# Pair 1 of an attention kernel loaded by tokens on GpSimd's queue, pair 0's x on the hardware queues, and all small tables from one diagonal

## The chip, the cores and the metric

The kernel runs on one core of a Trainium2 chip. The metric is device time in microseconds (us), lower is better. Three runs of the kernel before gave 121.71, 122.49 and 123.0; the median, 122.49, is the time before. A profile is one further execution, recorded by the hardware profiler.

The core has engines that run side by side, each with its own queue of instructions in program order: TensorE (matmul; PE in the profile, its weight loads PEld), VectorE (DVE), ScalarE (ACT), GpSimd (POOL) and SyncE (SP). Transfers between memory and the core are carried by 16 DMA engines. SyncE and ScalarE issue them to hardware queues (q1 and q10 in the profile), GpSimd to a software queue (q0); only GpSimd's transfers change the type on the way.

## What is computed

```python
batch, n_heads, seq, head_dim, d_state = (4, 8, 768, 32, 16)      # x, a, B, C
n_tokens, d_model, d_ff = (3072, 256, 1536)                       # w_a, w_b, w_out
...
    for c in range(nc):
        ...
        cum = np.cumsum(la, axis=-1)
        L = np.exp(cum[:, :, :, None] - cum[:, :, None, :])
        causal = np.arange(chunk)[:, None] >= np.arange(chunk)[None, :]
        L = L * causal
        CB = np.einsum('bhin,bhjn->bhij', Cc, Bc)
        M = CB * L
        y_intra = np.einsum('bhij,bhjd->bhid', M, xc)
        decay_to_i = np.exp(cum)
        y_inter = np.einsum('bhin,bhnd->bhid', Cc, state) * decay_to_i[:, :, :, None]
        y[:, :, sl] = y_intra + y_inter
        ...
        state = decay_full[:, :, None, None] * state + np.sum(Bx, axis=2)
...
    a = x @ w_a
    b = x @ w_b
    return (a * b @ w_out).astype(np.float32)
```

A linear attention with decay (state space form), whose output y, its heads side by side, is the input of a bilinear feed-forward layer. All inputs and the output are float32.

## The kernel before, in words

The sequence of 768 is cut into 6 blocks of 128 tokens, the batch of 4 into 2 pairs of sequences (bt is 0 or 1 within one). A *pair* p stands for block p // 2 and sequences 2(p % 2) and 2(p % 2) + 1, so there are 12 pairs. Each pair goes through these stages:

- Loads of B, C and x into the tiles bn, cn and xn (`load1`, `load2`, lines 134 to 154). For pairs below P0 = 4 a partition holds two neighbouring tokens of one sequence: partitions 0 to 63 are sequence 0, 64 to 127 sequence 1, and each load is two transfers with runs of 128 bytes (B, C) or 256 bytes (x). From pair 4 on a partition is a token ("by token"); runs are 64 bytes for B and C, 128 for x, and one transfer takes both sequences.
- `scale_bc` (line 314) multiplies B and C by the decay factors fB and fC, giving bm and cm in float16. `transposes` or, for pair 1, `transposes1` turn them on TensorE into BT and CT; from pair 4 on a DMA turns them. `scale_x` makes a float16 copy of x.
- `scores` (line 414) multiplies BT by CT into PSUM; `mask` (line 464) multiplies by the causal table while it copies to T1, three quarters on VectorE and one on GpSimd (there ScalarE copies out of PSUM first). The two-token layout uses the table `causal`, the by-token one `causal_q`.
- `pv_u` (line 477) and `ds_mm` (line 505) multiply by x to the output and the state sums. Pair 0's output goes by `evac0`, the others' by `pv`, to X2T, the input of the feed-forward layer.

The feed-forward layer of a pair runs in six units (`unit_mm`, line 658, for Wa and Wb, 256 columns a matmul; `evac_a` copies Wa's result; `times` multiplies), then by Wo. Units of the first pairs are interleaved with the next pairs' stages. From block 2 on both pairs of a block share units of 512 columns (`bunit`, line 735).

The decays come from `scan` (running product of a within a block), `over_mid` (reciprocal of its middle), `sel_over_mid`, and `factors_mm` (line 266), small float32 matmuls by the table `sel` that lay the factors out on the partitions.

Nothing is scheduled automatically: each engine's order is the program's order. Line 180 on issues the loads: a, B and C of pairs 0 and 1 by SyncE and ScalarE; then the tables are made, `sel`, `ident`, `headm` and `causal` by GpSimd's affine selects (lines 198 to 236), with reduces and copies on VectorE. Behind these on GpSimd's queue stand x of pair 0, the first half of Wa, the first quarter of Wb (lines 237 to 240) and x of pair 1; the rest of Wb's first half and the second halves of Wa and Wb follow at lines 855 and 856, after GpSimd's `scale_bc` of pair 1 and its `mask` of pair 0. The weights are cast to float16 on the way. Pair 2's inputs and Wo follow on the same queue (lines 878 to 885), pair 3's on SyncE after the second half of Wb (line 921). `warmup` (line 244) issues matmuls on zeros, whose result isn't used, while TensorE would otherwise wait at the start. `units_mm` runs the first two units of pair 0 with Wa, first both on the first half of X2T, then both on the second. PSUM banks of the pool `psf` are given out by the string BANKS, in the order of the calls.

Of the kernel before, what the change touches and what calls it, by code (L numbers as in the profile page):

```python
# [10 lines left out]
f32 = mybir.dt.float32  # L11
# [11 lines left out]
    "01232013201321023102310231023102301230120312031201320132013201320132031023102310213203120"  # L23
    "3120310213021302130210321032103210321032103210321302130213021302130213021302130213021302"
# [4 lines left out]
def kernel(  # L29
# [13 lines left out]
    nc = tc.nc  # L43
# [31 lines left out]
    zero = big.tile([BH, Q], f32, name="zero")  # L75
# [12 lines left out]
    warm = big.tile([128, 512], f16, name="warm")  # L88
# [41 lines left out]

    def by_token(t_):
        return t_.rearrange("p h r n -> p (h r n)").rearrange("p (t h n) -> p t h n", t=2, h=H)

    def load1(eng, p, which, bt, i0=0, n=64):
        blk, bp = divmod(p, NBP)
        if p >= P0:
            return eng.dma_start(
                by_token(pair_in[p][which])[:, bt],
                (B, C, x)[which][2 * bp + bt, :, blk * Q : (blk + 1) * Q, :].rearrange("h q n -> q h n"),
            )  # L140
# [6 lines left out]
    def load2(eng, p, which):  # L147
        if p < P0:
            return [load1(eng, p, which, bt) for bt in range(2)]
# [6 lines left out]
    def load_w(half):  # L156
        c = slice(half * KC, (half + 1) * KC)
        return [
            nc.gpsimd.dma_start(W[half], src.rearrange("(f p) e -> p f e", p=128)[:, :, c])
            for W, src in ((Wa, moe_w_a), (Wb, moe_w_b))  # L160
        ]

    def load_w0(which, part):
        W, src = ((Wa, moe_w_a), (Wb, moe_w_b))[which]
        w = (KC, KC // 2)[which]
        t_ = W[0][part] if which else W[0]
        nc.gpsimd.dma_start(t_, src.rearrange("(f p) e -> p f e", p=128)[:, :, part * w : (part + 1) * w])
# [13 lines left out]
    for p_ in range(3):  # L181
# [4 lines left out]
    load1(nc.sync, 0, 1, 0, 0, 32)  # L186
    load1(nc.scalar, 0, 1, 0, 32, 32)
    load1(nc.sync, 1, 0, 0)
    load1(nc.scalar, 1, 0, 1)
    load1(nc.sync, 1, 1, 0)  # L190
    load1(nc.scalar, 1, 1, 1)
    nc.scalar.preload_act_table_set("natural_log_exp_and_others")
    nc.vector.memset(warm.bitcast(u32), 0)
    nc.vector.memset(ident, 1.0)
    nc.vector.memset(headm, 1.0)
    nc.vector.memset(causal, 1.0)
    nc.vector.memset(zero, 0.0)
    nc.gpsimd.memset(sel, 1.0)
    nc.gpsimd.affine_select(
        out=sel,  # L200
        in_=sel,
        compare_op=ALU.is_equal,
        fill=0.0,
        base=0,
        pattern=[[-H, 2], [-2 * H, NBP], [-1, H]],
        channel_multiplier=1,
    )
    nc.gpsimd.affine_select(
        out=ident, in_=ident, compare_op=ALU.is_equal, fill=0.0, base=0, pattern=[[-1, 128]], channel_multiplier=1
    )  # L210
# [7 lines left out]
    nc.vector.tensor_copy(indm.rearrange("p (h n) -> p h n", n=N), of_h.unsqueeze(2).broadcast_to((BH, H, N)))  # L218
    for base, step in ((0, 1), (N - 1, -1)):
        nc.gpsimd.affine_select(  # L220
            out=headm,
            in_=headm,
            compare_op=ALU.is_ge,
            fill=0.0,
            base=base,
            pattern=[[-N * step, H]],
            channel_multiplier=step,
        )
    nc.vector.tensor_reduce(
        out=par, in_=headm.rearrange("p (m e) -> p e m", e=2), op=ALU.add, axis=mybir.AxisListType.X  # L230
    )
    for bt in range(2):
        v = causal[64 * bt : 64 * bt + 64]
        nc.gpsimd.affine_select(  # L234
            out=v, in_=v, compare_op=ALU.is_ge, fill=0.0, base=0, pattern=[[-1, 2], [1, Q]], channel_multiplier=-2
        )
    for bt in range(2):
        load1(nc.gpsimd, 0, 2, bt)
    load_w0(0, 0)
    load_w0(1, 0)  # L240
    for bt in range(2):
        load1(nc.gpsimd, 1, 2, bt)

    def warmup(n, bank, cols=512):
        for _ in range(n):
            nc.tensor.matmul(
                bank[:, 0:cols], warm[:, 0:128], warm[:, 0:cols], start=True, stop=True, skip_group_check=True
            )


    def scan(lo, hi):
        for k in range(lo, hi):
            nc.vector.tensor_tensor_scan(Pr[:, k], a_sb[:, k], zero, 1.0, ALU.mult, ALU.add)
# [12 lines left out]
    def factors_mm(lo, hi, fps=None, k0=0):  # L266
        if fps is None:
            fps = bank("fps")
        w = 2 * NBP * H
        F = fps[:, k0 * w : (k0 + hi - lo) * w].rearrange("p (k r c) -> p k r c", k=hi - lo, r=2)  # L270
        for k in range(lo, hi):
            for r in range(2):
                for bt in range(2):
                    nc.tensor.matmul(
                        F[64 * bt : 64 * bt + 64, k - lo, r],
                        Pr[:, k].rearrange("p (i r) -> p r i", r=2)[:, r],
                        selr[:, k, bt],
                        start=True,
                        stop=True,
                        skip_group_check=True,  # L280
                        tile_position=(0, 64 * bt),
                    )
        return F.rearrange("p k r c -> p (k r c)")

# [29 lines left out]
    def scale_bc(p, which, eng, factor=None):  # L314
        blk, bp = divmod(p, NBP)
        name, f = (("bm", fB), ("cm", fC))[which]
        raw = by_token(pair_in[p][which]) if p >= P0 else pair_in[p][which].rearrange("p h r n -> p r h n")
# [64 lines left out]
    def transposes1(which, T_):  # L382
# [8 lines left out]
        if which:  # L391
            CT = mid.tile([128, 2, Q], f16, name="ct", tag="ct")
            nc.vector.tensor_copy(
                CT.rearrange("p t (i r) -> p r (t i)", r=2), T_.rearrange("p (r c) -> p r c", r=2)
            )
            s["CT"] = CT
        else:
            BT = mid.tile([128, 2, 2, 2, 64], f16, name="bt", tag="bt")
            s["BT"] = BT
# [14 lines left out]
    def scores(p):  # L414
        BT, CT = st[p]["BT"], st[p]["CT"]
        st[p]["T1"] = mid.tile([128, H, 2, Q], f16, name="t1", tag="t1")
        for e, bt, m in itertools.product(range(2), range(2), range(4)) if p >= P0 else ():
# [11 lines left out]
        for e in range(2) if p < P0 else ():  # L429
# [15 lines left out]
    def product(p, m):  # L445

        if p >= P0:
# [29 lines left out]
    def pv_u(p, u, py, first):  # L477
# [12 lines left out]
        for r in range(2) if p < P0 else ():  # L490
# [14 lines left out]
    def ds_mm(p, c0, banks):  # L505
        s = st[p]
        s["DS"] = [b_[:, c0 : c0 + 2 * D] for b_ in banks]
        for bt, m in itertools.product(range(2), range(4)) if p >= P0 else ():
# [9 lines left out]
        for r in range(2) if p < P0 else ():  # L518
# [138 lines left out]

    def unit_mm(p, k2, W, kks=range(2), ps=None):
# [14 lines left out]

    def units_mm(p, ks, W, order):
        pss = {k2: bank("aps" if W is Wa else "bps") for k2 in ks}
        for k2, f in order:
            for kk in range(2):
                k = 2 * k2 + kk
                nc.tensor.matmul(  # L679
                    pss[k2][:, kk * 2 * Q : (kk + 1) * 2 * Q],  # L680
                    w_of(W, k, f),
                    X2T[:, p, :, f],
                    start=(f == 0 and kk == 0),
                    stop=(f == 1),
                    skip_group_check=True,
                )
        return [pss[k2] for k2 in ks]
# [121 lines left out]
    warmup(6, SC[3])  # L809
    warmup(2, SC[3], 128)  # L810
# [7 lines left out]
    v = factors_mm(0, 1, fps)  # L818
    nc.vector.reciprocal(flat(fB, 0, 1), v)
    warmup(1, SC[3])  # L820
    v1 = factors_mm(1, 2, bank("fps"))
    warmup(1, SC[3])
    scale_bc(0, 0, nc.vector)
    scale_bc(0, 1, nc.vector, v.rearrange("p (r b h) -> p r b h", r=2, b=NBP)[:, :, 0])
# [3 lines left out]
    nc.scalar.copy(flat(fC, 0, 1), v)  # L828
# [312 lines left out]
```

## Time and profile before

| | us |
|---|---|
| median of three runs (lowest, highest) | 122.49 (121.71, 123.0) |
| the profiled execution, its own time | 122.28 |
| its span, from first to last instruction | 120.5 |
| TensorE busy | 114.9 (95% of the span) |
| VectorE, ScalarE, GpSimd busy | 87.4, 73.2, 61.7 |
| hardware queue of SyncE: packets, MB | 62272, 9.31 |
| hardware queue of ScalarE: packets, MB | 2528, 0.36 |
| GpSimd's queue: packets, MB | 2448, 3.80 |
| first half of Wa, issue to landing | 7.1 |
| x of pair 0, issue to landing, each of two | 3.5 |
| second half of Wb, issue to landing | 8.3 |

A profile page gives busy times of the engines, the span in slices, the DMA queues, the chain of work that ended last, and groups of instructions with the mean time of one and what the engine waited for before it. A matmul's time runs from its start to a modelled end, so it overlaps the next one; a group of matmuls in a row shows the step between them. A group's releaser is the event that came last by the profile. In a timeline, the engine's name is followed by the line of the kernel, the operation, the tile written and the tiles read.

### The profile page before, as it was taken

How to read it: one execution, taken by the hardware profiler on the slowest of the kernel's cores; microseconds unless marked ns; L12 is line 12 of the kernel's file. 1: busy time of each engine (PE TensorE's matmuls, PEld its weight loads, DVE VectorE, ACT ScalarE, POOL GpSimd, SP SyncE). 2: the span in 40 equal slices, each digit the busy share in tenths (PEclk: the TensorE clock that was granted, in tenths of full speed). 3: DMA queues.
4: the chain of work that ended last, by engine and by line, in shares of the span. 5: the costliest groups of instructions: out<-in, count | busy, mean ns of one | idle time of the engine just before them, and what ended most of it. 6: DMA issues, size and time to landing. Idle time of an engine off the chain costs nothing.

```text
span 120.5 us, 3683 instructions
## 1 busy us (share of the span) xinstructions
PE 114.9 (95%) x1436; PEld 79.0 (66%) x1436; DVE 87.4 (72%) x175; ACT 73.2 (61%) x147; POOL 61.7 (51%) x107
## 2 busy tenths in 40 slices
PE   5996999999999999999999999999999999999990
PEld 2544899888888798645476464766464684655890
DVE  5988797995979888499984999577899435847100
ACT  0485867685875667787667737645646737566220
POOL 6998998981797586299822992177200000000200
PEclk9999999999999999999999999999999999999999
DMA  2999999969959899699688964995401012010032
GB/s 61 188 152 199 184 196 163 228 116 116 102 85 124 125 129 135 118 131 161 64 147 113 217 215 110 96 161 120 143 0 44 10 41 85 0 44 5 23 107 87
DMA packets 67265, 13.70 MB, mean 114 GB/s; under 512 B 62000, under 2 KB 66864, under 8 KB 67248
## 3 DMA queue, kind: packets, MB, share of 16 engines
q1 hardware_dynamic: 62272, 9.31, 47.6%
q0 software_dynamic: 2448, 3.80, 16.6%
q10 hardware_dynamic: 2528, 0.36, 1.8%
q8 instruction: 11, 0.18, 0.6%
q14 instruction: 6, 0.05, 0.1%
HBM read 11.11 MB, written 3.15 MB: 118 GB/s over the span
## 4 chain that ended last, share of the span: by engine, by line
PE 83%; DMA 10%; POOL 4%; issue 0%; DVE 0%; ACT 0%
PE ops L768 18%; PE aps L743 18%; PE bps L743 17%; PE ops L713 8%; PE bps L664 7%; PE aps L664 6%; DMA Wa<-in_moe_w_a_dram 6%; DMA turned<-planes 4%; PE SC L420 2%; PE SC L481 2%; POOL xn L142 1%; PE SC L495 1%; PE aps L679 1%; PE SC L570 1%; POOL causal L234 1%; PE SC L435 1%
## 5 line engine op out<-in xcount | busy, mean ns | idle before, releaser
L691 ACT COPY asb<-aps 128x512 f32<-128x512 f32 x72 | 41.7, 587 | 13.8 <-PE aps L743 9.6
L753 DVE TENSOR_TENSOR hkb<-bps,asb 128x512 f16<-128x512 f32 x48 | 32.3, 689 | 13.0 <-ACT asb L691 11.9
L743 PE MATMUL aps<-XB,Wa 128*128 128x512 f16 x96 | 28.6, 379 | 0.0
L743 PE MATMUL bps<-XB,Wb 128*128 128x512 f16 x96 | 28.5, 379 | 0.0
L768 PE MATMUL ops<-Wo,hkb 128*128 128x256 f16 (+1 forms) x204 | 22.5, 267 | 0.0
L768 PEld LDWEIGHTS <-hkb 128*128 128x128 f16 x204 | 18.5, 98 | 3.1
L475 DVE TENSOR_TENSOR t<-SC,causal_q 128x512 f16<-128x512 f32 x27 | 17.2, 682 | 3.3 <-PE SC L420 3.3
L698 DVE TENSOR_TENSOR hk<-bps,asb 128x512 f16<-128x512 f32 x24 | 16.2, 684 | 3.5 <-ACT asb L691 1.2
L743 PEld LDWEIGHTS <-Wb 128*128 128x128 f16 x96 | 9.9, 103 | 10.9
L743 PEld LDWEIGHTS <-Wa 128*128 128x128 f16 x96 | 9.7, 103 | 9.1 <-issue 0.2
L782 POOL DMA_DIRECT2D out_dram<-osb x1 | 0.6, 642 | 28.0 <-ACT osb L780 28.0
L780 ACT ACTIVATE osb<-ops 128x256 f32<-128x256 f32 (+1 forms) x16 | 6.0, 377 | 14.3 <-PE ops L768 14.2
L664 PE MATMUL bps<-X2T,Wb 128*128 128x256 f16 x96 | 13.8, 273 | 0.0
L664 PE MATMUL aps<-X2T,Wa 128*128 128x256 f16 x88 | 12.7, 273 | 0.0
L713 PE MATMUL ops<-Wo,hk 128*128 128x256 f16 x96 | 11.5, 273 | 0.0
L473 POOL TENSOR_TENSOR t<-tmp,causal_q 128x512 f16<-128x512 f32 x5 | 5.8, 1160 | 8.6 <-ACT tmp L472 8.5
L664 PEld LDWEIGHTS <-Wb 128*128 128x128 f16 x96 | 9.8, 103 | 0.6
L713 PEld LDWEIGHTS <-hk 128*128 128x128 f16 x96 | 8.9, 98 | 1.4
L312 POOL TENSOR_SCALAR x<-xn 128x512 f16<-128x512 f32 x6 | 8.9, 1491 | 1.3 <-DMA xn<-in_x_dram 0.8
L319 POOL TENSOR_TENSOR planes<-cn,fC 128x256 f16<-128x256 f32 x8 | 5.0, 622 | 8.8 <-DMA cn<-in_C_dram 8.7
L664 PEld LDWEIGHTS <-Wa 128*128 128x128 f16 x88 | 8.9, 103 | 0.6
L327 POOL TENSOR_TENSOR bm<-bn,fB 128x256 f16<-128x256 f32 x11 | 6.9, 623 | 2.6 <-PE aps L664 1.1
(112 smaller groups left out, 128.7 us busy)
## 6 DMA issues: line engine op xcount, KB each, us to landing
out_dram<-osb SPq DMA_DIRECT2D x22, 128.0 KB, 1.8
xn<-in_x_dram SPq DMA_DIRECT2D x6, 256.0 KB, 4.0
cn<-in_C_dram SPq DMA_DIRECT2D x8, 128.0 KB, 4.1
bn<-in_B_dram SPq DMA_DIRECT2D x8, 128.0 KB, 4.1
xn<-in_x_dram POOLq DMA_DIRECT2D x6, 128.0 KB, 6.4
Wa<-in_moe_w_a_dram POOLq DMA_DIRECT2D x2, 384.0 KB, 7.1
Wo<-in_moe_w_out_dram POOLq DMA_DIRECT2D x2, 384.0 KB, 6.9
xn<-in_x_dram SPq DMA_DIRECT2D x4, 128.0 KB, 4.5
```

The source lines that it names most:

```text
L312: eng.tensor_scalar(xo, xi, XS, None, ALU.mult)
L327: eng.tensor_tensor(out=m_, in0=raw, in1=(of_pair(f, blk, bp) if factor is None else factor).unsqueeze(3).broadcast_to((128, 2, H, N)), op ...
L473: nc.gpsimd.tensor_tensor(out=o_, in0=tmp, in1=c_, op=ALU.mult)
L475: nc.vector.tensor_tensor(out=o_, in0=i_, in1=c_, op=ALU.mult)
L664: nc.tensor.matmul(ps[:, kk * 2 * Q : (kk + 1) * 2 * Q], w_of(W, k, f), X2T[:, p, :, f], start=(f == 0), stop=(f == 1), skip_group_check=True,
L691: (nc.vector.tensor_copy if on_dve else nc.scalar.copy)(asb, a_ps)
L698: nc.vector.tensor_tensor(out=s["hk"][:, 2 * k2 : 2 * k2 + 2, :].rearrange("p k q -> p (k q)"), in0=b_ps, in1=asb, op=ALU.mult)
L713: nc.tensor.matmul(o_ps[:, 0:d_model], hk[:, k, bt * Q : (bt + 1) * Q], Wo[:, k, :], start=(k == 0), stop=(k == NK - 1), skip_group_check= ...
L743: nc.tensor.matmul(t_, w_of(W, k, f), XB[:, blk - P0 // NBP, f].rearrange("p t j q -> p (t j q)"), start=(f == 0), stop=(f == 1), skip_gro ...
L753: return lambda: nc.vector.tensor_tensor(out=s["hk"][:, k], in0=ps[1], in1=asb, op=ALU.mult)
L768: nc.tensor.matmul(o_ps[:, 0:w], hk[:, k, c * Q : (c + 1) * Q], Wo[:, k, cs], start=(k == 0), stop=(k == NK - 1), skip_group_check=True,)
L780: nc.scalar.activation(out=o_sb[:, 0:w], in_=o_ps[:, 0:w], func=AF.Copy, scale=1.0 / (YS * YS))
```

## The change

- Pair 1 is loaded and computed by token, as the pairs from 4 on are (`tok`): B, C and x each in one transfer on GpSimd's queue; TensorE still turns its B and C. Its scores, `pv_u` and `ds_mm` take half as many matmuls of full height. Its masks use `causal_q`. Its factors for block 0 come from a matmul of their own (`factors_mm1`).
- Pair 0's x goes to the queues of ScalarE and SyncE, behind its C; C is no longer cut in three.
- GpSimd makes only `ident`, then issues B and C of pair 1 and the first half of Wa, then makes half of `causal`, then issues the first quarter of Wb, x of pair 1 and the next quarter of Wb. The second halves of Wa and Wb are issued after the pool's mask of pair 0, now ahead of pair 0's product in the program.
- `sel`, `causal_q`, `headm` and `par` come from `ident` on VectorE (a copy, a scan and two reduces); ScalarE copies `indm` and the other half of `causal`.
- The zeros of `zero`, now on 128 partitions, serve the warmup matmuls; their numbers change.
- cm of pair 1 is made on VectorE ahead of pair 0's last mask, both second evacuations of pair 0 go to ScalarE, pair 1's CT is made before pair 0's second product, and the first units of pair 0 run one after the other (`half_mm` is defined and not called). BANKS follows the new order of the calls.

```diff
+    def tok(p):
+        return p == 1 or p >= P0
...
-    load1(nc.sync, 0, 1, 0, 0, 32)
-    load1(nc.scalar, 0, 1, 0, 32, 32)
-    load1(nc.sync, 1, 0, 0)
-    load1(nc.scalar, 1, 0, 1)
-    load1(nc.sync, 1, 1, 0)
-    load1(nc.scalar, 1, 1, 1)
+    load1(nc.sync, 0, 1, 0)
+    load1(nc.scalar, 0, 2, 1)
+    load1(nc.sync, 0, 2, 0)
     nc.scalar.preload_act_table_set("natural_log_exp_and_others")
-    nc.vector.memset(warm.bitcast(u32), 0)
     nc.vector.memset(ident, 1.0)
-    nc.vector.memset(headm, 1.0)
-    nc.vector.memset(causal, 1.0)
     nc.vector.memset(zero, 0.0)
-    nc.gpsimd.memset(sel, 1.0)
-    nc.gpsimd.affine_select(
-        out=sel,
...
+    nc.vector.memset(causal[0:64], 1.0)
     nc.gpsimd.affine_select(
         out=ident, in_=ident, compare_op=ALU.is_equal, fill=0.0, base=0, pattern=[[-1, 128]], channel_multiplier=1
+    )
+    nc.vector.tensor_copy(sel, ident[0:BH, 0:BH].rearrange("p (b t h) -> p t b h", b=NBP, t=2))
+    nc.vector.tensor_tensor_scan(causal_q, ident, zero, 0.0, ALU.add, ALU.add)
+    nc.vector.tensor_reduce(
+        out=headm, in_=ident.rearrange("p (h n) -> p h n", n=N), op=ALU.add, axis=mybir.AxisListType.X
+    )
...
-    for bt in range(2):
-        load1(nc.gpsimd, 0, 2, bt)
-    load_w0(0, 0)
-    load_w0(1, 0)
-    for bt in range(2):
-        load1(nc.gpsimd, 1, 2, bt)
+    load2(nc.gpsimd, 1, 0)
+    load2(nc.gpsimd, 1, 1)
+    load_w(0, 0)
+    nc.gpsimd.affine_select(
+        out=causal[0:64],
...
+    load_wb0(0)
+    load2(nc.gpsimd, 1, 2)
+    load_wb0(1)
...
+    def factors_mm1(fps):
+        F = fps[:, 4 * H : 6 * H]
+        nc.tensor.matmul(
+            F, Pr[:, 0], selr[:, 0, :, H : 2 * H], start=True, stop=True, skip_group_check=True
+        )
+        return F.rearrange("p (t h) -> p t h", t=2)
...
-    warmup(6, SC[3])
-    warmup(2, SC[3], 128)
+    warmup(5, SC[3])
+    nc.scalar.copy(indm.rearrange("p (h n) -> p h n", n=N), of_h.unsqueeze(2).broadcast_to((BH, H, N)))
+    nc.scalar.copy(causal[64:128], causal[0:64])
     scan(0, 1)
...
-    v = factors_mm(0, 1, fps)
-    nc.vector.reciprocal(flat(fB, 0, 1), v)
+    v = factors_mm(0, (0,), fps)
+    nc.vector.reciprocal(fB[:, 0, :, 0], v)
...
+    v01 = factors_mm1(fps1)
+    nc.vector.reciprocal(fB[:, 0, :, 1], v01)
...
     mask(product0(1, 1), by_pool=True)
+    scale_bc(1, 1, nc.vector)
+    load_w(1, 0)
+    w1 = load_w(1, 1)
     scale_x(0, nc.scalar)
     mask(product0(1, 0))
-    warmup(3, tcp)
+    warmup(5, tcp)
     part = transposes1(0, bank("tb"))
     part(0)
-    warmup(2, tcp)
-    scale_bc(1, 1, nc.vector)
+    warmup(1, tcp)
...
+    transposes1(1, SC[0])
     part(1)
-    warmup(1, tcp)
     pv_u(0, 1, py, True)
-    transposes1(1, SC[0])
     for bt in range(2):
-        evac0(1, bt, (nc.scalar, nc.vector)[bt], py)
-    load_w0(1, 1)
-    w1 = load_w(1)
+        evac0(1, bt, nc.scalar, py)
+    scan(5, NBLK)
     scores(1)
-    scan(5, NBLK)
-    over_mid(2, NBLK)
-    mask(product(1, 3), by_pool=True)
+    mask(product(1, 3), by_pool=True, by_token=True)
+    aps = [unit_mm(0, 0, Wa)]
+    asb = [evac_a(aps[0])]
+    for k2 in range(1, 3):
+        aps.append(unit_mm(0, k2, Wa))
+    for m in range(3):
+        mask(product(1, m), by_token=True)
+        if m == 0:
+            over_mid(2, NBLK)
+    scale_x(1, nc.scalar)
+    asb.append(evac_a(aps[1]))
...
-    nc.gpsimd.memset(causal_q, 1.0)
-    nc.gpsimd.affine_select(
-        out=causal_q, in_=causal_q, compare_op=ALU.is_ge, fill=0.0, base=0, pattern=[[1, Q]], channel_multiplier=-1
-    )
```

## The prediction

> **What bounds the kernel now.** The chain of waits was read first. In the extract, the columns are start, length and what ran, in us.
>
> ```profile
> 2.94 1.52 POOL xn L142 x2
> 4.46 7.06 DMA Wa<-in_moe_w_a_dram
> 11.52 0.05 issue
> 11.57 1.05 PE aps L679 x8
> ...
> 36.60 4.73 DMA turned<-planes
> 41.33 0.05 issue
> ```
>
> GpSimd's setup and its two issues of pair 0's x end at 4.46; the first half of Wa is issued then and lands at 11.52; TensorE starts its long run at 11.57. After that the chain is TensorE alone, except where it meets the turned planes of pair 5 at 41.33.
>
> Second, the timeline around the start (start, length, engine, line, work, idle before).
>
> ```profile
> 9.15 0.75 POOL L167 DMA_DIRECT2D Wb<-in_moe_w_b_dram  x1
> 10.49 0.28 DVE L612 TENSOR_SCALAR X2T<-py 128x128 f16<-128x128 f32 x1
> 10.65 0.43 PE L435 MATMUL SC<-ct,bt 32*64 32x128 f16 x32 [0.53 <-DVE ct L393]
> 11.57 1.05 PE L679 MATMUL aps<-X2T,Wa 128*128 128x256 f16 x8 [0.49 <-DMA Wa<-in_moe_w_a_dram]
> 13.11 0.63 ACT L310 ACTIVATE x<-xn 128x512 f16<-128x512 f32 x1
> 19.16 0.70 POOL L142 DMA_DIRECT2D xn<-in_x_dram  x1 [0.44 <-DMA Wb<-in_moe_w_b_dram]
> ```
>
> X2T of pair 0 is complete at 10.77, TensorE idles 0.49 for Wa. So an earlier Wa alone is worth 0.5. The last two lines show that more arrivals are just in time. Pair 1's x lands at 13.1 (issued at about 6.6, landing time 6.6) and is scaled at once; pv(1) follows at 13.80. Pair 2's last x issue waits until 19.16 for the second half of Wb (landed about 19.0); pair 2's bm and cm stand behind it on GpSimd, done at 21.09, and TensorE's weight load for transposing bm starts at 21.27, some 0.2 later.
>
> Third, stretches of time with the share of the DMA engines (column before the last) and GB/s (last).
>
> ```profile
> 2.40:6.80 4.40, 4.22 (x32) 2.22 (x31) 3.75 (x15) 2.09 (x5) 4.33 (x8) 1.00 1.01 181
> 6.80:7.60 0.80, 0.78 (x34) 0.48 (x34) 0.48 (x2) 0.42 (x4) 0.73 (x2) 1.00 0.86 75
> 11.00:12.00 1.00, 0.51 (x18) 0.42 (x5) 0.97 (x4) 0.59 (x1) 0.44 (x2) 1.00 0.98 133
> 12.00:16.50 4.50, 4.50 (x102) 4.00 (x101) 3.59 (x7) 3.42 (x8) 4.33 (x8) 1.00 1.13 187
> ```
>
> The DMA engines are full from 2.4 on. So the opening and the next 10 us are one queue of transfers (Wa, Wb's first part, pair 1's x, more Wb, Wa, Wb), and TensorE can be early only by as much as that queue is early. Two stretches are slack: 6.8 to 7.6, where Wa's data only starts, and 11 to 12, after GpSimd issued Wb's next part only at 9.15, behind a mask.
>
> **The change, part by part.**
>
> *GpSimd's order.* The selects for sel, headm and one half of causal go (0.25 + 2 x 0.2 + 0.43), and two issues of x. ident's memset is first on VectorE, so its select can run at about 1.15 to 1.44, and the two by-token issues follow. Their price is shown once before, for x of pair 8 with the same 2048 runs:
>
> ```profile
> 53.14 1.23 POOL L151 DMA_DIRECT2D xn<-in_x_dram  x1
> ```
>
> 512 runs cost 0.73 (x, B and C of pairs 0 to 2). Between 0.73 and 1.23 I take 1.23, the row of that shape. Wa's issue then begins at 1.42 + 2 x 1.23 = 3.88 instead of 4.46 (by 0.73 at 2.88; it is no earlier if each takes (4.46 - 1.42) / 2 = 1.52). Next: half a causal select 0.43, Wb 0.74, x of pair 1 1.23, Wb 0.74, to 7.1 + 0.7 = 7.8; Wb's second part begins at 7.1, not 9.15. bm of pair 1 moves from 7.39 to 7.8, the pool's mask of pair 0 from 8.04 to 8.4. The second halves of Wa and Wb follow that mask at 9.6, as before (9.88).
>
> The Trainium skill, "DMA: Bandwidth & Descriptors", section "Anatomy of one DMA", calls descriptor generation a small cost of which many can be had before it shows. The pair 8 row disagrees: four times the runs took 0.5 longer. By the page Wa would be issued a microsecond earlier than by the row.
>
> *Work for the DMA engines.* Traffic of 128 B runs on a hardware queue alone moved 1237 in 1 us, 64 B runs 1668, 256 B runs 460: per engine 12.9 and 9.6 ns, and 18 ns of busy time for 256 B.
>
> ```profile
> q1 hardware_dynamic: 1668, 0.11, 113.3%
> ```
>
> On GpSimd's queue pair 8's x (128 B) cost 8.0 ns a run (share of three windows, 59.4 + 39.2 + 3.8% of 16 engines for 2048 runs), and 256 B runs 14.4 (pair 1's x in the 0.92 us at 10 to 11). No row has 64 B there. It lies between 4 (half of 8.0, bytes alone) and 9.6 (the hardware row); I take 8.0 x 9.6 / 12.9 = 5.9, scaled by the two hardware rows. Ahead of Wa: before 4096 x 12.9 / 16 + 1024 x 14.4 / 16 = 4.2 us; after 2048 x 12.9 / 16 + x of pair 0 on hardware 1024 x 18 / 16 + 4096 x 5.9 / 16 = 4.3 (3.8 to 5.3). So there is no less to move. Pair 1's x costs 2048 x 8.0 / 16 = 1.0 for 0.9 (1.65 by the hardware row). What is won is slack: Wa, issued earlier, can start while x of pair 0 still moves, so the 0.8 at 75 GB/s instead of 175 (0.45 lost) mostly fills, taken as 0.4; and Wb's second part is queued in time, so 11 to 12 no longer loses 1 - 133/187 = 0.28. Sum: Wa lands 0.3 earlier (0.1 - 0.4), pair 1's x 0.2, the last of Wb 0.5 (-1.2 to +1.7).
>
> *Pair 0's chain.* Its x goes behind C on both hardware queues; the issues of pair 1's B and C there go. When GpSimd's data joined at 4.7, the hardware transfers issued 1.7, 1.4 and 0.9 before took 0.7, 0.8 and 1.5 longer. The first packet of pair 0's x came at 4.7, 1.8 after its issue; so GpSimd's data now joins at 3.2 to 3.3, and C (issued 1.54 and 2.04, landed at 4.95 at the latest) lands at up to 5.5, where cm wants it at 5.42: 0.1 lost. x lands by 7.5, wanted at 7.86: hidden. The first reciprocal is on 16 columns for 32: -0.1. VectorE's new setup (scan 0.4, reduces, copies: some 1.3 after ident, from 1.45) is done before a lands at 2.9. indm and causal's other half go to ScalarE, idle till 5.99; the copy waits for the select that ends at 5.1, with pair 0's bt queued behind it: hidden by 0.5. The second reciprocal goes in VectorE's 0.32 wait at 7.39. cm of pair 1 now stands ahead of pair 0's last mask, waiting for C of pair 1 (issued 2.65, landing after the 5.1 of pair 8's x: 7.75, wanted 8.65); that mask ends at 9.7 instead of 9.28 and its product starts 0.3 later, but both evacuations are now on ScalarE ahead of the scan and copy that held VectorE, so X2T is complete at about 10.7 (10.5 to 11.2). It does not bind if Wa lands at 11.2.
>
> *TensorE.* pv and state sums of pair 1 take half the matmuls: 0.34 + 0.14 against 0.28 + 0.06 (half of 0.56 and 0.12 of later pairs): -0.14, after pv(1) has waited for x. The order of the first units changes without a price.
>
> *Sum.* Start -0.3. At pv(1) the wait for x leaves -0.2, less the 0.14 saved: -0.3. At pair 2's transposes the last of Wb (-0.5) allows it. Pair 3's and 4's loads also follow Wb, so the idle 0.13 at 41.33 goes: -0.4 in all. The profiled run had 122.28 (span 120.5 and 1.8 around it): 121.9. The median of the three is 0.2 above it, so 122.0 to 122.1; I say 122.0. Its own range, 121.4 to 122.7, is Wa and x a half microsecond either way.
>
> **The rivals.**
>
> *The queue gets well ahead* (64 B at 4 ns, Wa by its issue time). TensorE starts as soon as X2T is there, 10.65 for 11.57, and pair 1 and the wait at 41.33 add 0.14 + 0.13: -1.2, 121.1, or 121.3 against the median. For it: Wa's landing time of 7.06 includes 256 KB queued ahead, and the second part of Wb took 4.8. Against: bytes are the same and the engines were full.
>
> *Small runs fill the queue.* If runs on GpSimd's queue cost what they do on hardware, B and C of pair 1 add 4096 x 9.6 / 16 - 2048 x 12.9 / 16 = 0.8, its x 0.7, pair 0's x 0.2: the last Wb lands 1.7 later, at 20.7, and pair 2's bm, cm and transposes with it. Less the 0.2 margin and pair 1's 0.14: +1.4, 123.7, 123.9 against the median. It decides from 0.3 of delay at the last Wb. For it: the hardware rows; against: the 8.0.
>
> *The clock rises late.* At the start a 512-column warmup step took 0.43, from about 5.4 on 0.22.
>
> ```profile
> 1.25 2.96 PE L246 MATMUL SC<-warm 128*128 128x512 f16 x8 [1.25 <-DVE warm L193]
> 7.19 0.82 PE L246 MATMUL tc<-warm 128*128 128x512 f16 x3
> ```
>
> TensorE was busy without a break from 1.25. Five steps now end near 3.45 and it idles till the factors at 4.1. If the rise is put off again and again by new gaps and the run starts slow, some 4 us (as long as the rise took) at half speed lose 2, less 0.5 of cover: +1.5, 123.8, 124.0 against the median. Against: gaps of 0.5 at 10.65 and 11.57 did no harm. The Trainium skill, "TensorE: Matmul & The Clock Gate", section "Part 1: The HAM clock gate", has the rate rise after one sustained busy window of some 3.4 us of a free-running count. The first five steps alone would not fill one; the trace's rise came after about 4 us of work. By the page a break costs one more window, as an estimate over by some 9, ahead of the long run, and the sum would stay as forecast.
>
> *The change doesn't do what it says:* Wa is not issued earlier if the two issues exceed 1.52 each; this is a part of the second rival.
>
> **How the numbers follow.** A measurement here tells about 1% (1.2 us) from no change. Forecast 0.40 (0.05 of it beyond -1%); queue well ahead 0.28, which lies on the bound, 0.20 beyond it; small runs 0.19, of it 0.16 slower; late clock 0.13, of it 0.12 slower. Faster 0.25, same 0.47, slower 0.28. The range 121.0 to 123.9 leaves out some 0.08 below and 0.09 above.
>
> **What would show it.** Wa's issue near 3.9 and its landing near 11.2; 1.2 per by-token issue; no dip in GB/s at 7 and at 11; pair 1's x at 12.9; Wb's last at 18.5; 256-column steps at 0.11 from the first unit. The forecast is wrong if Wa lands after 11.6 or before 10.7, if C or x holds pair 0 so that X2T is later than 11.3, or if TensorE shows new gaps between 14 and 42.

## The result, and the profile after

Six runs of the changed kernel gave a median of 124.53 us (124.05 to 125.17), six of the kernel before 122.48 (121.71 to 123.5): a ratio of 1.0148, 95% interval 1.0108 to 1.0188. The change costs 2 us, and the time lies above the forecast's range. The profiled execution took 124.70, its span 123.0 against 120.5. Ratios compare undisturbed runs only, while a median is over all runs, and two experiments' profiles (the select first with the opening warmups of before, and the diagonal alone) show a granted clock of about 0.50 for some us from 11.5 on, so no length of TensorE's work is read from them there.

The chain of waits of the changed kernel (start, length, what ran; `...` stands for lines left out):

```profile
1.27 0.72 SPq L144
2.04 4.73 DMA cn<-in_C_dram
6.87 0.43 DVE cm L321
...
8.81 0.58 PE SC L427 x24
9.40 2.25 PE tc L232 x5
...
12.28 0.42 PE py L497 x12
12.70 0.28 ACT X2T L612
13.02 0.58 PE py L497 x16
...
13.93 1.57 PE aps L677 x12
```

Wa's first half is gone from the chain, as intended. In its place stands C of pair 0, SyncE's half: issued at 2.04, landed at 6.77, where before both halves were there by 4.95. TensorE starts its long run at 13.9, not 11.57 (it stands at 13.93 in the chain and at 13.86 in the timeline, where the matmul before it still overlaps). From there the chain is TensorE alone: the wait for the turned planes at 41.33 is gone too. Wo's 72 last matmuls start at 113.42 instead of 111.12, so of the 2.5 in the span 2.3 come from TensorE's late start; the other 0.2 is behind its last matmul, in the last output's store.

The timeline around the start (start, length, engine, line, work, idle before it and what ended that):

```profile
1.43 1.35 POOL L153 DMA_DIRECT2D bn<-in_B_dram  x1
2.78 1.16 POOL L153 DMA_DIRECT2D cn<-in_C_dram  x1
3.92 0.73 POOL L167 DMA_DIRECT2D Wa<-in_moe_w_a_dram  x1
...
6.87 0.42 DVE L321 TENSOR_TENSOR cm<-cn,fps 128x256 f16<-128x256 f32 x1 [1.50 <-DMA cn<-in_C_dram]
...
9.33 2.31 PE L232 MATMUL tc<-zero 128*128 128x512 f16 x5
...
10.22 1.16 POOL L465 TENSOR_TENSOR t<-tmp,causal 128x512 f16<-128x512 f32 x1 [0.94 <-ACT tmp L464]
10.71 0.95 DVE L321 TENSOR_TENSOR cm<-cn,fC 128x256 f16<-128x256 f32 x1
11.32 0.77 POOL L167 DMA_DIRECT2D Wa<-in_moe_w_a_dram  x1
11.59 0.68 DVE L467 TENSOR_TENSOR t<-SC,causal 128x512 f16<-128x512 f32 x1
12.08 0.72 POOL L167 DMA_DIRECT2D Wb<-in_moe_w_b_dram  x1
13.86 1.64 PE L677 MATMUL aps<-X2T,Wa 128*128 128x256 f16 x12
```

VectorE waits 1.50 for C before it makes cm of pair 0 (5.53 before, 6.87 now), and all of pair 0 stands behind that. Then cm of pair 1 takes 0.95 instead of 0.42 beside GpSimd's mask, so pair 0's last mask starts at 11.59 and ends at 12.27. The chain doesn't pass through that mask, though: from the scores on it is TensorE's own work, the five late warmups in 2.25 above all, and one wait for ScalarE's copy into X2T. Wa was issued at 3.92 and landed 6.0 later, at 9.92: TensorE had its weights for 4 us before it had X2T. The second halves of Wa and Wb, behind GpSimd's mask, are issued at 11.32 and 12.08, so the DMA engines run dry in between.

What the queues moved in 3.6 to 4.8 us (packets, MB, share of 16 engines), before and after:

```profile
q1 hardware_dynamic: 801, 0.10, 53.2%
q10 hardware_dynamic: 689, 0.08, 45.7%
q0 software_dynamic: 1, 0.00, 2.3%
```

```profile
q0 software_dynamic: 29, 0.12, 82.1%
q10 hardware_dynamic: 241, 0.03, 16.7%
q1 hardware_dynamic: 25, 0.00, 1.8%
```

On the hardware queues a packet here is one run; on GpSimd's it is 4 KB, 64 runs. These 29 packets took 0.821 x 1.2 x 16 = 15.8 us of engine time, 0.54 each, 8.5 ns a run. The hardware queues, which carried all that pair 0 was waiting for, moved 266 runs instead of 1490.

### The profile page after: what moved, and what is told of

It reads as the page before. It is cut to its first block, busy times and chain, and to the rows that moved or that the text cites. A ratio compares the mean times of both kernels' runs of the same rounds, so it can differ in the third digit from the quotient of the medians.

```text
span 123.0 us, 3588 instructions
## 1 busy us (share of the span) xinstructions
PE 117.2 (95%) x1393; PEld 79.6 (65%) x1393; DVE 88.1 (72%) x175; ACT 74.3 (60%) x150; POOL 60.8 (49%) x99
## 4 chain that ended last, share of the span: by engine, by line
PE 91%; DMA 4%; SPq 1%; ACT 0%; DVE 0%; issue 0%; DVEq 0%
PE ops L766 18%; PE aps L741 17%; PE bps L741 17%; PE ops L711 9%; PE aps L677 9%; PE bps L677 9%; DMA cn<-in_C_dram 4%; PE SC L412 2%; PE tc L232 2%; PE SC L473 2%; PE SC L427 1%; PE py L497 1%; PE SC L572 1%; SPq L144 1%; PE SC L497 1%; PE SC L232 0%
## 5 line engine op out<-in xcount | busy, mean ns | idle before, releaser
L467 DVE TENSOR_TENSOR t<-SC,causal_q 128x512 f16<-128x512 f32 x30 | 19.1, 680 | 3.5 <-PE SC L412 3.5
L741 PEld LDWEIGHTS <-Wa 128*128 128x128 f16 x96 | 9.7, 103 | 9.1 <-issue 0.2
L677 PE MATMUL aps<-X2T,Wa 128*128 128x256 f16 x96 | 13.8, 273 | 0.0
L711 PE MATMUL ops<-Wo,hk 128*128 128x256 f16 x96 | 11.5, 273 | 0.0
L465 POOL TENSOR_TENSOR t<-tmp,causal_q 128x512 f16<-128x512 f32 x6 | 7.0, 1159 | 8.6 <-ACT tmp L464 8.5
L677 PEld LDWEIGHTS <-Wa 128*128 128x128 f16 x96 | 9.6, 103 | 1.0 <-issue 0.2
```

The costliest lines, as they stand in the source:

```text
L465: nc.gpsimd.tensor_tensor(out=o_, in0=tmp, in1=c_, op=ALU.mult)
L467: nc.vector.tensor_tensor(out=o_, in0=i_, in1=c_, op=ALU.mult)
L677: nc.tensor.matmul(ps[:, kk * 2 * Q : (kk + 1) * 2 * Q], w_of(W, k, f), X2T[:, p, :, f], start=(f == 0), stop=(f == 1), skip_group_check=True,
L711: nc.tensor.matmul(o_ps[:, 0:d_model], hk[:, k, bt * Q : (bt + 1) * Q], Wo[:, k, :], start=(k == 0), stop=(k == NK - 1), skip_group_check= ...
L741: nc.tensor.matmul(t_, w_of(W, k, f), XB[:, blk - P0 // NBP, f].rearrange("p t j q -> p (t j q)"), start=(f == 0), stop=(f == 1), skip_gro ...
```

## The experiments

All kernels compute the whole result. Two theories stood first: that pair 1's by-token packets on GpSimd's queue, in the DMA engines by 3.6 us where GpSimd's first data came at 4.7 before, hold C of pair 0 back; and that x of pair 0, now on the hardware queues behind C, does. Beside them the late warmup matmuls (2.31 us) could be a cost of their own.

**Wa ahead of the by-token loads.**

```diff
+    load_w(0, 0)
     load2(nc.gpsimd, 1, 0)
     load2(nc.gpsimd, 1, 1)
-    load_w(0, 0)
```

> The changed kernel with one step moved: on GpSimd's queue the first half of Wa is issued ahead of pair 1's B and C by token, not behind them. In the changed kernel the second half of pair 0's C (SyncE's queue, issued 2.04) landed at 6.8, VectorE waited 1.5 us for it, and the long run on TensorE began at 13.86. Theory 1 (the by-token packets of 64 runs of 64 bytes, some 0.6 us each on a DMA engine, shut the hardware queues out at 4.0 to 4.8): without them before 5 us C lands by 5.7, VectorE's wait for it is under 0.4, the run begins at 12.4 or earlier, and the time falls by 1.0 to 2.0 us, to 122.5 to 123.5. Theory 2 (x of pair 0 on the hardware queues holds C up): C still lands after 6.3 and the time stays within 0.5 of 124.5. Theory 3 (TensorE's clock rises late for want of warmup work, whatever C does): C may be early, but the warmup steps of 512 columns still take 0.43 until about 11 and the time falls by less than 1.

Measured: 126.73, ratio 1.0331 (1.0246 to 1.0417). Its timeline:

```profile
7.67 0.42 DVE L321 TENSOR_TENSOR cm<-cn,fps 128x256 f16<-128x256 f32 x1 [1.95 <-DMA cn<-in_C_dram]
10.29 0.61 POOL L321 TENSOR_TENSOR bm<-bn,fB 128x256 f16<-128x256 f32 x1 [2.70 <-DMA bn<-in_B_dram]
13.28 0.63 ACT L304 ACTIVATE x<-xn 128x512 f16<-128x512 f32 x1 [2.39 <-DMA xn<-in_x_dram]
15.43 1.63 PE L677 MATMUL aps<-X2T,Wa 128*128 128x256 f16 x12
```

With Wa's data in front C comes no sooner but later, at 7.6, and B of pair 1 and x of pair 0 are late as well. In 3.6 to 4.8 us GpSimd's queue had 77.0% of the engines and the hardware queues moved 114 runs. (That B is on GpSimd's queue itself, behind Wa.) So it is not the by-token packets alone: Wa's data, joining early on GpSimd's queue, pushes the hardware loads back as well. The chain of this kernel goes through x of pair 0, which landed at 13.2.

**Both halves of pair 0's x on SyncE's queue.**

```diff
-    load1(nc.scalar, 0, 2, 1)
     load1(nc.sync, 0, 2, 0)
+    load1(nc.sync, 0, 2, 1)
```

> The changed kernel with both transfers of pair 0's x on SyncE's queue behind C, none on ScalarE's, so that no x can run beside the second half of C. Theory 2: C of sequence 0 lands about 1 us earlier, at 5.8 or before, and the time falls by 0.8 or more. Theory 1: C still lands after 6.2, because the stretch without hardware traffic at 4.0 to 4.8 stays; x lands later (8.5), and the time stays within 0.5 of 124.5. Theory 3: within 0.5 of 124.5.

Measured: 124.66, 1.0153 (1.0072 to 1.0234). C landed at 6.74 and cm waited 1.48, as in the changed kernel; the long run began at 13.82. Where x stands makes no difference to C, so the second theory falls.

**No late warmup matmuls.**

```diff
-    warmup(5, tcp)
...
-    warmup(1, tcp)
```

> The changed kernel without the six warmup matmuls between scores(0) and the first product of pair 0 (five ahead of the transpose of pair 1's B, one behind it). In the changed kernel those five took 2.31 us at the low clock and pair 0's product began at 12.21, though its masks were done at 10.8 and x at 10.6. Theory 3 in the form that these steps at the low clock stand in the way: the product begins at about 11.0, the long run 1 to 1.3 earlier at 12.6 to 12.9; but if it then starts at the low clock it loses again up to 1.7. Theory 1: the wait for C at 5.4 to 6.9 stays at 1.5 in any case; of the 2.3 us by which the run began later than before, no more than 1.2 can come back here.

Measured: 126.22, 1.0288 (1.0214 to 1.0361). The product of pair 0 was at 10.58 instead of 12.21, but the last mask (11.49 to 12.17) held its second half, and the long run began only 0.74 earlier, at 13.12, and slowly, by this line of the timeline:

```profile
13.12 2.74 PE L677 MATMUL aps<-X2T,Wa 128*128 128x256 f16 x12
```

Twelve matmuls took 2.74 where the changed kernel needs 1.64. The warmups cost at most 0.74 of the start and are worth more than that.

**The causal select first.** GpSimd makes its half of `causal` ahead of the by-token issues, so that its data joins some 0.7 us later (B of pair 1 is issued at 2.12 instead of 1.43). Nothing else is moved.

```diff
+    nc.gpsimd.affine_select(
+        out=causal[0:64],
...
     load2(nc.gpsimd, 1, 0)
     load2(nc.gpsimd, 1, 1)
     load_w(0, 0)
-    nc.gpsimd.affine_select(
-        out=causal[0:64],
...
```

> The changed kernel with the causal select (0.44) ahead of the by-token issues on GpSimd's queue, so that their data join about 0.45 later, at 4.1 instead of 3.65. Theory 1: C, which needs some 0.3 to 0.5 us more of the engines at 3.65, is mostly through; it lands 0.5 to 1.0 earlier (5.8 to 6.3) and the time falls by 0.5 to 1. Theory 2: C lands as before, at 6.8, or no more than 0.2 earlier. Theory 3: no change in time beyond 0.4.

Measured: 123.03, 1.0032 (0.9957 to 1.0107). The same queues in 3.6 to 4.8 us, and the timeline:

```profile
q10 hardware_dynamic: 660, 0.13, 53.8%
q1 hardware_dynamic: 504, 0.06, 33.5%
q0 software_dynamic: 3, 0.01, 3.0%
```

```profile
4.60 0.73 POOL L167 DMA_DIRECT2D Wa<-in_moe_w_a_dram  x1
...
5.44 0.42 DVE L321 TENSOR_TENSOR cm<-cn,fps 128x256 f16<-128x256 f32 x1 [0.17 <-DMA cn<-in_C_dram]
...
9.29 0.41 DVE L321 TENSOR_TENSOR cm<-cn,fC 128x256 f16<-128x256 f32 x1
9.37 1.35 POOL L465 TENSOR_TENSOR t<-tmp,causal 128x512 f16<-128x512 f32 x1
...
11.85 1.63 PE L677 MATMUL aps<-X2T,Wa 128*128 128x256 f16 x12
```

The hardware queues move 1164 runs, C lands at 5.34, cm waits 0.17, and the long run starts 2.0 earlier. The span is 120.8, 2.2 less than after; this execution was the fastest of its four, and by the ratios (1.0032 for 1.0148) the select first is worth 1.4. Of the 2.0, cm of pair 0 brings 1.43 (5.44 for 6.87). The other 0.58 lies between cm of pair 0 and the long run, which took 6.41 here and 6.99 in the changed kernel. There TensorE's steps had become short in time: the single late warmup took 0.38 at 10.07, for 0.63 at 11.65 in the changed kernel. That cm of pair 1 now takes 0.41 for 0.95, because it starts 0.08 ahead of GpSimd's mask and not behind it, was not on the changed kernel's chain. C is no longer cut in three in either kernel, so the missing cut can be worth no more than the 0.4 by which it still lands after the 4.95 of before.

This one reordering takes back most of what the change lost, and Wa's data in front made C later still: GpSimd's early join is the cause of that part.

**Select first, with the opening warmups of before (six of 512 columns and two of 128); the same warmups alone; and the pool's mask ahead of bm of pair 1.**

```diff
-    warmup(5, SC[3])
+    warmup(6, SC[3])
+    warmup(2, SC[3], 128)
```

```diff
-    scale_bc(1, 0, nc.gpsimd)
...
     mask(product0(1, 1), by_pool=True)
+    scale_bc(1, 0, nc.gpsimd)
```

> The kernel with the select first (C of pair 0 landed at 5.3, the long run began at 11.85, 123.03) with the opening warmups as they were before the change, six of 512 columns and two of 128 instead of five of 512. There the clock rose only at about 9.7, and the five later warmups took 2.21. Theory 3 (the clock rose late because TensorE idled from 3.4 to 3.75 and had less to do): the rise is back at 5 to 6, the five later steps take 1.1 to 1.3, the long run begins at 10.9 to 11.4 and the time is 122.0 to 122.6. If the rise is a matter of chance of the start and not of the opening steps: it stays near 9.7 and the time within 0.4 of 123.0.

> The changed kernel with only the opening warmups as before the change (six of 512 and two of 128). Theory 1 with theory 3 as a second cause: C still lands at about 6.8 and VectorE waits 1.4 to 1.5 for it, scores(0) begins at about 8.3; the clock rises by 6, the later five steps take 1.1 instead of 2.3 and the long run begins about 1.3 to 1.6 earlier, at 12.3 to 12.6: 122.9 to 123.3. If TensorE's wait for C lets the clock fall again or keeps it low: the steps still take 2.1 or more and the time stays at 124.1 to 124.8.

> Select first and opening warmups as before the change, and on GpSimd the mask of pair 0 ahead of bm of pair 1, which waited for B of pair 1 (landed 8.6) with the mask queued behind it. Theories 1 and 3 together: the pool's mask ends at about 9.3 instead of 10.7, the second halves of Wa and Wb are not held by it any longer than bm; X2T of pair 0 is complete at 10.6 to 11.2, the long run begins at 10.9 to 11.2, and the time is 121.3 to 122.2, at or below the kernel before. If bm's later end holds TensorE's transpose (in order ahead of pair 0's product), no gain on the kernel without the swap, within 0.3 of it.

Measured: select first with the warmups 122.98, 0.9974 (0.9934 to 1.0014); the warmups alone on the changed kernel 124.31, 1.0124 (1.0065 to 1.0183); select first, the warmups and the mask ahead 124.72, 1.0154 (1.0073 to 1.0235). The late warmups in the timelines of the first and of the third:

```profile
7.11 1.25 PE L232 MATMUL tc<-zero 128*128 128x512 f16 x5
```

```profile
8.26 2.31 PE L232 MATMUL tc<-zero 128*128 128x512 f16 x5
```

The same opening, the same earlier loads, and TensorE's step is 0.22 in one profiled execution and 0.43 in the other. So the opening warmups don't decide when the rate rises. Alone, they left it low as well (2.31 at 9.06; C landed at 6.5, and the long run began at 13.51). In the first, with the rate up, the long run began at 11.18, the earliest of all; what that is worth can't be read from its profile, whose granted clock was 0.57 in 11.5 to 12 and 0.50 after that. The third kernel's loss is therefore not settled as the mask's: its bm and cm of pair 1 were late (11.09 and 10.61) and its clock stayed low.

**The kernel before, with x of pair 0 issued ahead of GpSimd's selects.** Here GpSimd's data joins early in the old kernel, with runs of 256 bytes.

```diff
+    for bt in range(2):
+        load1(nc.gpsimd, 0, 2, bt)
     for base, step in ((0, 1), (N - 1, -1)):
         nc.gpsimd.affine_select(
             out=headm,
...
-    for bt in range(2):
-        load1(nc.gpsimd, 0, 2, bt)
     load_w0(0, 0)
```

> The kernel before the change, with one step moved: on GpSimd's queue the two issues of pair 0's x (runs of 256 bytes, 16 to a packet) stand ahead of the selects for headm and causal, so that their data join the hardware queues about 1.2 us earlier, at 3.4 instead of 4.7. Theory 1 as a matter of joining early (any GpSimd traffic that starts before C is through holds C): C of pair 0, landed at 4.95 before, lands at 5.7 or later, VectorE waits for it, and the time is 0.3 to 1.0 above the kernel before. Theory 1 as a matter of the packets of 64 runs (0.6 us each, against 0.24 for 16 runs): C lands by 5.4 and the time is within 0.3 of the kernel before, or lower by up to 0.4.

Measured: 123.45, 1.0056 (1.0024 to 1.0088). The queues in 3.6 to 4.8 us:

```profile
q0 software_dynamic: 63, 0.19, 43.8%
q10 hardware_dynamic: 581, 0.07, 38.6%
q1 hardware_dynamic: 295, 0.04, 19.5%
```

A packet of GpSimd's queue now takes 0.438 x 19.2 / 63 = 0.13 us, a quarter of a by-token one, and the hardware queues still move 876 runs. C landed at 5.54 and 5.7, 0.8 later than before; the change made it 1.8 to 2.0. No wait for C shows, since VectorE waited 1.20 for `headm` first, whose selects now stand behind the issues, and TensorE's step was still long (0.61 for a single 512-column matmul at 6.40). So this kernel's time can't be laid to C, and it gives the price of the early join only through C's landing.

**cm of pair 1 behind pair 0's last mask, on top of the select first; and with three late warmups instead of five.**

```diff
-    scale_bc(1, 1, nc.vector)
...
-    warmup(5, tcp)
+    warmup(3, tcp)
...
     warmup(1, tcp)
+    scale_bc(1, 1, nc.vector)
```

> Select first (C on time, long run at 11.85, 123.03), and cm of pair 1 on VectorE back behind pair 0's last mask, as before the change. In the changed kernel cm, ahead of that mask, took 0.95 beside the pool's mask instead of 0.42, and the mask ended at 12.27. If that order costs (a second, smaller theory beside theory 1): the last mask ends 0.4 or more earlier, the long run begins 0.2 to 0.4 earlier, 122.6 to 122.9. If pair 0's second product waits for the pool's mask (ended 10.7) anyway: the long run within 0.1 and the time within 0.3 of the kernel with the select first.

> The same with three warmups instead of five between scores(0) and the transpose of pair 1's B, as before the change. With the select first the five ended at 10.1 while bm of pair 1 was done at 9.41, so TensorE came 0.55 late. Theory 3 in its second form (steps at the low clock stand in the way): the transpose begins at 9.4 to 9.5, the long run 0.3 to 0.6 earlier than with five, the time 122.0 to 122.6. If the fewer steps keep the clock low longer: the long run starts with steps of 0.21 per 256 columns, and the time is 123.5 or more.

Measured: 123.42, 1.0030 (0.9995 to 1.0064), and 123.58, 1.0005 (0.9959 to 1.0050). From the timeline of the first, with five late warmups:

```profile
5.37 0.42 DVE L321 TENSOR_TENSOR cm<-cn,fps 128x256 f16<-128x256 f32 x1
...
7.88 2.31 PE L232 MATMUL tc<-zero 128*128 128x512 f16 x5
...
12.37 1.65 PE L677 MATMUL aps<-X2T,Wa 128*128 128x256 f16 x12
```

Pair 0's masks were done at 9.95, and still cm of pair 0 and the long run are 7.00 apart, as in the changed kernel (6.99): what they share is the low rate. The second began its long run at 11.48; then x of pair 1 was 0.45 late, and between 20 and 40 TensorE was busy in 18.61 of 20.00 us, where GpSimd waited 4.2 for C of a later pair. Neither differs from the select first by more than the intervals.

**The kernel before with the tables from one diagonal.** Only the tables are changed, so GpSimd issues x of pair 0 from 2.12 and Wa at 3.67; pair 1 stays on the hardware queues.

```diff
+    nc.vector.tensor_copy(sel, ident[0:BH, 0:BH].rearrange("p (b t h) -> p t b h", b=NBP, t=2))
+    nc.vector.tensor_tensor_scan(causal_q, ident, zero, 0.0, ALU.add, ALU.add)
...
     for bt in range(2):
         load1(nc.gpsimd, 0, 2, bt)
     load_w0(0, 0)
```

> The kernel before with only the tables changed: all from one diagonal as in the changed kernel, the causal select behind it, then on GpSimd pair 0's x, the first half of Wa, Wb and pair 1's x as before; loads of pair 1 stay in the two-token layout on the hardware queues. Wa is issued about 0.8 earlier (3.7), x joins at about 3.9 to 4.0, with 256-byte runs. Theory 1: C lands at 5.0 to 5.4 and is hardly waited for (with the select first it was 5.34, waited 0.17); Wa lands 0.5 to 0.8 earlier, the long run begins at 11.1 to 11.2 instead of 11.57, and the time is 0.2 to 0.5 below the kernel before. If any earlier start on GpSimd's queue costs the opening more than it brings: at or above the kernel before.

Measured: 1.0128 (1.0034 to 1.0223), from two of its six runs, 124.07 and 125.18; the median of the six is 126.09. The profiled execution took 126.15, so it shows which loads come late and not what that costs. Its timeline, pair 1's B and C:

```profile
9.31 0.62 POOL L319 TENSOR_TENSOR bm<-bn,fB 128x256 f16<-128x256 f32 x1 [2.77 <-DMA bn<-in_B_dram]
...
11.75 0.43 DVE L319 TENSOR_TENSOR cm<-cn,fC 128x256 f16<-128x256 f32 x1 [2.20 <-DMA cn<-in_C_dram]
```

The same mechanism with another victim: GpSimd's x and Wa come early, and now B and C of pair 1, last on the hardware queues, are waited for, 2.77 and 2.20. Freeing GpSimd sooner was thus no gain by itself here; it was paid by what the hardware queues still held.

**All that helped, together:** select first, opening warmups of before, cm behind the last mask, three late warmups.

> All that helped in its place, put together: the causal select ahead of the by-token issues, cm of pair 1 behind pair 0's last mask, three late warmup matmuls instead of five, and the opening warmups of the kernel before (six of 512 columns, two of 128). If only the early traffic of GpSimd's queue cost the time, and the rest of the change is worth what its parts showed (Wa 0.6 earlier, pv of pair 1, the idle at 41.33): the long run begins at about 11.1 to 11.3 and the ratio to the kernel before is 0.990 to 0.997. If the time the clock takes to rise, which the opening does not fix, takes back what is won: 0.997 to 1.005, as for the three select-first kernels so far.

Measured: 123.26, 1.0017 (0.9979 to 1.0055). Its timeline:

```profile
7.20 0.82 PE L232 MATMUL tc<-zero 128*128 128x512 f16 x3
...
8.59 0.62 POOL L321 TENSOR_TENSOR bm<-bn,fB 128x256 f16<-128x256 f32 x1 [0.68 <-DMA bn<-in_B_dram]
8.70 0.63 ACT L304 ACTIVATE x<-xn 128x512 f16<-128x512 f32 x1 [0.74 <-DMA xn<-in_x_dram]
9.17 1.15 POOL L465 TENSOR_TENSOR t<-tmp,causal 128x512 f16<-128x512 f32 x1
9.20 1.41 DVE L321 TENSOR_TENSOR cm<-cn,fC 128x256 f16<-128x256 f32 x1
...
11.66 1.49 PE L677 MATMUL aps<-X2T,Wa 128*128 128x256 f16 x12
```

In this execution TensorE's rate was up by the late warmups (0.82 for three), and still the long run began at 11.66. Now pair 0's x and pair 1's B are 0.7 late, and cm of pair 1 falls right behind GpSimd's mask and takes 1.41. Wa landed at 11.0, half a microsecond earlier than before, but X2T, by way of these loads and that mask, was complete only at 11.70, where before it was at 10.77. So the earlier Wa was worth nothing here. No version tried beats the kernel before by more than the intervals; five of the six with the select first lie between 0.997 and 1.003 of it.

## Why the prediction was wrong

**The step that failed** is that of pair 0's chain: C "lands at up to 5.5, where cm wants it at 5.42: 0.1 lost". It landed at 6.77, and cm waited 1.50. The mechanism was named rightly, that GpSimd's data joins sooner and the hardware transfers in flight take longer; its size was taken from x of pair 0 in the kernel before, which has runs of 256 bytes. With such runs the early join cost C 0.8 (the kernel before with x early); with the by-token packets it cost 1.8 to 2.0, and with Wa's data, which joined half a microsecond sooner still, 2.6 to 2.8. The sum had no term for what GpSimd's traffic leaves to the hardware queues, which moved 876, 266 and 114 runs in 3.6 to 4.8 us in these three. Its own test, "if C or x holds pair 0 so that X2T is later than 11.3", is what came true: X2T was complete at 14.1.

**cm of pair 1 ahead of the last mask** was priced at its usual 0.42. Beside GpSimd's mask it took 0.95, and the last mask moved by that. It did not set the start: TensorE, with its late warmups at the low rate, came to the second product at 13.02, 0.75 after that mask. Only without the late warmups was the mask waited for (0.21, by the product at 12.23).

**The price of a 64-byte run** on GpSimd's queue, taken at 5.9 ns in a range of 4 to 9.6, was 8.5. The rival that small runs fill the queue had its price about right and its place wrong: it saw the loss at the last Wb and pair 2. The last Wb landed at 19.0, as before, and pair 2's transposes (23.75 for 21.38) are no later than the start has made all of TensorE's work; the loss fell on pair 0.

**The late clock** was a rival at +1.5, and the sum put it at nothing. In the changed kernel the 512-column step was still 0.43 past 11; the rise by some 9 that the prediction had estimated didn't come. Between cm of pair 0 and the long run lie 6.99 us in the changed kernel and 7.00 with C on time (select first, cm behind the mask), both at the low rate; 6.41 where the rate rose at about 9.7 (select first); 5.76 where it was up by 4.7 (5.42 to 11.18, select first with the opening warmups). The kernel before took 6.04, of them 0.49 in the wait for Wa. So of the 2.3 by which the profiled execution starts late, 1.34 is C's and 0.95 lies in this stretch, where the low rate is what the two long ones share. What the rate costs in the median stays open: the kernel before was profiled once, and when its rate rises in other executions isn't known. With C on time and the low rate, the start was 0.8 later than before and the ratio 1.003.

**Right** were Wa's issue (3.88 forecast, 3.92), the by-token issues (1.23 each forecast; 1.35, 1.16 and 1.21), pair 1's pv, state sums and the small product behind them (0.94 before, 0.80, hence -0.14), the end of the wait at 41.33, and TensorE without gaps from 14 on. Wa's landing was not: 9.92 for 11.2, below the 10.7 that the prediction named as a sign of being wrong, at a time when the hardware loads moved little. Stretches of the changed kernel, DMA share and GB/s in the last two columns, show the dip that was forecast to vanish at 11:

```profile
6.80:8.80 2.00, 1.46 (x13) 0.79 (x21) 1.67 (x5) 0.23 (x3) 0.94 (x3) 1.00 1.18 183
11.00:12.00 1.00, 1.00 (x5) 0.41 (x3) 1.00 (x2) 0.11 (x1) 1.00 (x2) 1.00 0.89 137
12.00:14.00 2.00, 1.94 (x52) 0.98 (x52) 0.90 (x4) 1.53 (x6) 0.81 (x2) 1.00 0.67 51
```

At 7 it is filled: 183 GB/s in 6.8 to 8.8, where the kernel before had 75 in 6.8 to 7.6. From 11 to 14 it is wider, since the second halves of the weights wait for a mask that pair 0 has delayed. These gains were worth 0.2: 0.14 at pair 1, and 0.08 between Wo's first long stretch and the one ahead of block 2 (22.74 us for 22.82). As much was lost on the way, 0.16 of it in the first twelve Wa matmuls (13.86 to 15.34, before 11.57 to 12.89), so Wo's last matmuls are late by the same 2.3 as the start.

## What to carry to other kernels

A software-queue transfer that is moved forward competes with every hardware load still in flight, so look at what those loads feed before freeing its issuing engine sooner; a delay of 0.7 us here, one table made first, was worth 1.2% of the kernel. Price such a collision with a row of the same kind of transfer beside hardware loads, by what it leaves to them: neither the bytes that the newcomer moved in 3.6 to 4.8 us (0.19, 0.12 and 0.08 MB) nor the time of one of its packets (0.13, 0.54 and 0.27 us) rises with the 0.8, 1.8 to 2.0 and 2.6 to 2.8 by which C was late; the runs left to the hardware queues (876, 266 and 114) fall with it. When a wait on weights is removed, follow the other input of the same matmul to see what the earlier weights can be worth at all.

## What was not expected of the hardware

The DMA engines don't share by bytes between a software and a hardware queue, and not by a fixed number of runs either. In 3.6 to 4.8 us the hardware queues moved 9.2 runs for each packet of GpSimd's beside by-token packets (266 / 29), 13.9 beside x's larger runs (876 / 63), and 2.1 with Wa in front (114 / 54). In 4.0 to 4.8, with all three in full flow, it was 3.7 (59 / 16), 11.4 (613 / 54) and 0.9 (41 / 45). The Trainium skill, "DMA: Bandwidth & Descriptors", section "Queues, rings and completion order", has each engine turn from queue to queue a packet at a time, typically 9 to 17 descriptors long and 64 at most. The by-token packet of 64 runs agrees with the limit. Taking a hardware run as one descriptor, and both hardware queues together, only the 11.4 lies in the typical range; the 3.7 and the 0.9 do not.

VectorE's product of two inputs in on-chip memory and GpSimd's mask don't run side by side, they take turns: behind the mask, cm ended 0.28 after the mask's end in the changed kernel, 0.28 with cm behind the last mask, 0.29 in the last kernel (0.95, 0.67 and 1.41 long), and where cm was 0.08 ahead, the mask took 1.35 for 1.15. The Trainium skill, "SBUF — State Buffer", section "SBUF: two separate sides", calls this an exclusive lock of a shared port, and these rows agree.

TensorE's rate rose at a time that the program doesn't fix. By the steps of the warmups, with one and the same opening it was up by 4.7 and by 5.7 in two executions (select first with the warmups, and the last kernel) and still low past 11 in two others, while the column of the granted clock showed 1.00 throughout those stretches. Busy time doesn't settle it either: with the mask ahead TensorE was busy without a gap from 1.26 to 10.5, and the step was still 0.43 at the end of it.
